# One feed-forward stage's first products by Strassen's scheme: seven block products in the place of eight

## The chip, the cores and the metric

The kernel runs on one core of one Trainium2 chip. The metric is the device time of one execution in microseconds (us); the runs of the kernel before were 1035.34 us in the median of 3 (1034.44 to 1036.2).

## The reference: what is computed

Attention over 4 x 8 heads, 576 positions, head size 64, with a decay and a causal mask; its output is 2304 tokens of 512 features. Two feed-forward stages follow on the same tokens, all in float32:

```python
def _moe_ref(x, w_in, w_out):          # stage 1: 512 -> 2048 -> 512
    h = x @ w_in
    g = h * (1.0 / (1.0 + np.exp(-h)))
    return g @ w_out

def _moe2_ref(x, w_a, w_b, w_out):     # stage 2: 512 -> 1536 -> 512
    a = x @ w_a
    b = x @ w_b
    return a * b @ w_out
```

"First products" are x @ w_in in stage 1 and x @ w_a and x @ w_b in stage 2; "second products" are those with w_out. The change concerns the first products of stage 2, a matrix of 2304 x 512 times two of 512 x 1536.

## The kernel before, in words

**Number format.** Every float32 operand of a feed-forward product is held as two float32r tiles, a rounded high part and the rest (`hi`, `lo`), and each product is three matmuls: high by high, high by low, low by high (`mm3`, L327 to L331). The weights come from DRAM as 8-byte numbers and are turned into `hi` and `lo` on the way, 256 columns at a time (`decode`, L278): one DMA, two ScalarE operations, four VectorE operations (L292, L293, L295, L297), two GpSimd operations (L299, L300).

**Tiling.** The 128 x 128 weight tile is the stationary operand, and up to 512 tokens move through it. The hidden features are cut into chunks: CH1 has seven for stage 1 (the last, chunk 6, has 2 tiles of 128 features), CH2 six for stage 2, of 2 tiles each. For each chunk the loop at L890 walks over the five token blocks of BLOCKS (four of 512, one of 256). Per block it issues the first products (`ff_in`, over 4 slices of the 512 input features, for each tile and, in stage 2, for each of the two matrices), then the second products of the block before (`ff_out`, 4 output slices by the chunk's tiles), then up to three decode steps for the next chunk. `ff_in` puts ScalarE's copy or tanh of the PSUM bank, VectorE's multiplication, ScalarE's cast to `ghi` and VectorE's subtraction for `glo` behind the products; `ff_out` adds the PSUM bank to the accumulator `acc` on VectorE (L383, L392).

**Order.** Attention and the first chunk are put in order by a planner (`Plan`): it lists the operations with modelled durations, schedules each engine by priority (`prio`), and the program issues them in that order. A row of random seeds (SHAKES) perturbs the priorities, so that another row gives another order. From chunk 1 on the order is that of the loop at L890, which no planner touches. Each engine executes its instructions in the order of issue. All loads and stores are issued by SyncE on one queue.

**Memory.** `x` holds the stage's input for all tokens as high and low parts, `accs` its sums in two halves of the tokens (TAIL = 1152). At the end of stage 1 `add_out` casts the sums back into `x`. PSUM has eight banks of 512 columns: four `s`, two `t`, one `pv`, one `mm`.

## Time and profile before

| what | value |
|---|---|
| median of 3 runs | 1035.34 us (1034.44 to 1036.2) |
| the profiled execution's own time | 1035.05 us |
| its span, first to last instruction | 1033.3 us |
| busy TensorE matmul, of the span | 1017.3 us, 98% |
| busy VectorE | 655.7 us, 63% |
| busy ScalarE | 439.6 us, 43% |
| busy GpSimd | 335.0 us, 32% |
| granted TensorE clock | 1.00 throughout |

Busy time of an engine counts the time in which at least one of its instructions is under way. Matmuls are pipelined: a row of one gives more than the engine needs before the next one can start, so a matmul's price is read from the distance of two starts. The same holds to a lesser degree on VectorE. 1.75 us of the profiled execution's time lie outside its span.

### The profile page before, as it was taken

To read this page: it belongs to the slowest core of one execution; us is meant where nothing else is said; L and a number is where in the kernel's file an instruction comes from. 1 tells how busy PE (TensorE), PEld (TensorE's weight loads), DVE (VectorE), ACT (ScalarE), POOL (GpSimd) and SP (SyncE) were. 2 spreads that over 40 slices of the span, in tenths; PEclk is the share of its full clock that TensorE was granted. 3 is DMA by queue.
4 is the path that set the end of the run, shared out by engine and by line. 5 is a ranking of instruction groups with operands and counts; after the bars stand their busy time and mean duration, and the time that the engine had idled before them with its cause. 6 is when DMAs were issued, how large, how long until landed. Compare 5 with 4: busy or idle time off the path is not lost.

```text
span 1033.3 us, 16115 instructions
## 1 busy us (share of the span) xinstructions
PE 1017.3 (98%) x5783; PEld 844.4 (82%) x5783; DVE 655.7 (63%) x1544; ACT 439.6 (43%) x1075; POOL 335.0 (32%) x414
## 2 busy tenths in 40 slices
PE   8999999999999999999999999999999999999998
PEld 6667777898788888888888788888888888888887
DVE  8896656557886857847649966176385475473334
ACT  5888788954334324423225445342232231231111
POOL 6574434333423403304006863061150250250000
PEclk9999999999999999999999999999999999999999
DMA  5443332211220201201101222021021030020012
GB/s 165 153 147 102 114 109 86 68 60 57 61 70 28 86 11 40 84 1 51 31 1 43 60 62 82 1 74 50 1 82 41 8 95 22 21 62 1 11 71 102
DMA packets 34096, 62.33 MB, mean 60 GB/s; under 512 B 7005, under 2 KB 8685, under 8 KB 33985
## 3 DMA queue, kind: packets, MB, share of 16 engines
q1 hardware_dynamic: 33904, 60.87, 19.1%
q8 instruction: 45, 0.74, 0.3%
q10 hardware_dynamic: 112, 0.45, 0.2%
q14 instruction: 35, 0.28, 0.1%
HBM read 56.05 MB, written 5.23 MB: 59 GB/s over the span
## 4 chain that ended last, share of the span: by engine, by line
PE 85%; DVE 7%; ACT 3%; DMA 3%; issue 1%; SPq 0%; POOL 0%; DVEq 0%; ACTq 0%; POOLq 0%
PE ps L329 14%; PE ps L330 14%; PE ps L331 14%; PE po L329 10%; PE po L330 9%; PE po L331 9%; PE s L582 4%; PE pv L702 3%; PE t_x L658 2%; PE t_y L658 2%; DMA d<-in_w 2%; ACT p L616 1%; DVE acc L383 1%; PE po L784 1%; PE po L785 1%
## 5 line engine op out<-in xcount | busy, mean ns | idle before, releaser
L330 PE MATMUL ps<-x,whi 128*128 128x512 f32 (+1 forms) x760 | 279.7, 368 | 0.0
L329 PE MATMUL ps<-x,whi 128*128 128x512 f32 (+1 forms) x760 | 279.6, 368 | 0.0
L331 PE MATMUL ps<-x,wlo 128*128 128x512 f32 (+1 forms) x760 | 279.6, 368 | 0.0
L299 POOL TENSOR_TENSOR d<-d,whi 128x256 f32<-128x256 f32 x116 | 97.9, 848 | 418.2 <-ACT whi L298 382.9
L329 PE MATMUL po<-ghi,whi 128*128 128x512 f32 (+1 forms) x520 | 189.6, 369 | 2.7 <-ACT ghi L361 2.7
L330 PE MATMUL po<-glo,whi 128*128 128x512 f32 (+1 forms) x520 | 191.6, 368 | 0.6 <-DVE glo L362 0.6
L331 PE MATMUL po<-ghi,wlo 128*128 128x512 f32 (+1 forms) x520 | 191.3, 368 | 0.0
L331 PEld LDWEIGHTS ps<-x,wlo 128*128 128x128 f32 x760 | 143.2, 188 | 23.9
L329 PEld LDWEIGHTS ps<-x,whi 128*128 128x128 f32 x760 | 143.3, 189 | 23.7
L330 PEld LDWEIGHTS ps<-x,whi 128*128 128x128 f32 x760 | 143.3, 189 | 23.7
L361 ACT CAST ghi<-g 128x512 fp32r<-128x512 f32 (+1 forms) x130 | 74.8, 575 | 141.0 <-DVE g L360 94.8
L329 PEld LDWEIGHTS po<-ghi,whi 128*128 128x128 f32 x520 | 97.9, 189 | 19.9 <-ACT ghi L361 3.8
L330 PEld LDWEIGHTS po<-glo,whi 128*128 128x128 f32 x520 | 98.0, 189 | 17.4 <-DVE glo L362 1.1
L331 PEld LDWEIGHTS po<-ghi,wlo 128*128 128x128 f32 x520 | 98.0, 188 | 16.2
L360 DVE TENSOR_TENSOR g<-g,ps 128x512 f32<-128x512 f32 (+1 forms) x60 | 37.9, 631 | 114.7 <-PE ps L331 114.3
L362 DVE TENSOR_TENSOR glo<-g,ghi 128x512 fp32r<-128x512 f32 (+1 forms) x130 | 88.2, 678 | 34.7 <-ACT ghi L361 34.2
L291 ACT ACTIVATE d<-d 128x256 f32<-128x256 f32 x116 | 50.6, 436 | 122.5 <-DMA d<-in_w 97.6
L300 POOL TENSOR_TENSOR wlo<-d,d 128x256 fp32r<-128x256 f32 x116 | 91.0, 789 | 34.6 <-DVE d L297 31.6
L383 DVE SCALAR_TENSOR_TENSOR acc<-po,acc 128x512 f32<-128x512 f32 (+3 forms) x144 | 76.0, 551 | 23.5 <-PE po L331 23.0
L292 DVE TENSOR_SCALAR d<-d 128x256 uint32<-128x256 uint32 x116 | 44.9, 387 | 69.4 <-ACT d L291 68.8
L392 DVE TENSOR_TENSOR acc<-po,acc 128x512 f32<-128x512 f32 (+2 forms) x120 | 64.6, 554 | 25.5 <-PE po L331 25.0
L359 ACT COPY g<-ps 128x512 f32<-128x512 f32 (+1 forms) x60 | 32.4, 540 | 103.1 <-PE ps L331 103.1
(129 smaller groups left out, 1490.6 us busy)
## 6 DMA issues: line engine op xcount, KB each, us to landing
d<-in_w SPq DMA_DIRECT2D x124, 256.0 KB
qk<-in_qk SPq DMA_DIRECT2D x15, 608.0 KB
vt<-in_v SPq DMA_DIRECT2D x16, 320.0 KB
rb<-invs SPq DMA_DIRECT2D x32, 128.0 KB
out_t<-acc SPq DMA_DIRECT2D x12, 256.0 KB
d2ghi<-in_w SPq DMA_DIRECT2D x8, 256.0 KB
e<-in_w SPq DMA_DIRECT2D x4, 256.0 KB
out_t<-acc SPq DMA_DIRECT2D x4, 192.0 KB
```

The costliest lines, as they stand in the source:

```text
L291: nc.scalar.activation(m, high.bitcast(F32), AF.Copy, scale=2.0 ** -112)
L292: nc.vector.tensor_scalar(m.bitcast(U32), m.bitcast(U32), 3, None, ALU.logical_shift_left)
L299: nc.gpsimd.tensor_sub(m, val, hi.bitcast(F32))
L300: nc.gpsimd.tensor_add(lo, m, e)
L329: nc.tensor.matmul(ps, wh, mh, start=start, stop=False)
L330: nc.tensor.matmul(ps, wh, ml, start=False, stop=False)
L331: nc.tensor.matmul(ps, wl, mh, start=False, stop=stop)
L361: nc.scalar.copy(ghi[:, t, :n], g)
L362: nc.vector.tensor_sub(glo[:, t, :n], g, ghi[:, t, :n].bitcast(F32))
L383: nc.vector.scalar_tensor_tensor(a, ps, 0.5, a, ALU.mult, ALU.add)
L392: nc.vector.tensor_add(a, ps, a)
L582: nc.tensor.matmul(out, stat, b[:, k0 + j0:k0 + j0 + nj], start=step == 0, stop=step == 3)
```

## The change: what it does, and the diff

Chunks 1 to 5 of stage 1 stay in the loop at L890. From chunk 6 on everything is issued by a second planner section.

- **Chunk 6** (`finish_first`): the same products, for six token blocks of 384 in the place of four of 512 and one of 256.
- **Stage 2, first products** (`third`): for a token block of 768 (two times 384, one from each half of the tokens), 512 input features (two times 256) and 256 hidden features (two tiles), each of the two matrices is multiplied as a 2 x 2 by 2 x 2 product of blocks in the Winograd form of Strassen's scheme: seven block products (TERMS) of 6 matmuls each where the plain form has eight. The order is SPOTS: the products of the two matrices in turn (a0 b0 a1 b1 ...), and at each "." one output slice of the second products of the sweep before. Some products accumulate in the same PSUM bank, with a copy of the bank taken on ScalarE between (k = 0, 2, 3, and 5 of the first matrix), and are finished by VectorE additions (`close`). Three sweeps, one for each block of 768 tokens, cover 256 hidden features; 18 sweeps cover the stage, and the direction of the blocks turns with each set of weights.
- **Terms of x** (`build`): the seven left operands of a block are sums of accumulator slices, made on VectorE, split into high and low on ScalarE and VectorE or GpSimd (`low_part`). They are made once per block in the first three sweeps. Two sets of slots lie in what was `x`; blocks 0 and 2 share one, so their terms are saved to a DRAM tile (`cache`) and fetched again by DMA (`save`, `fetch`: 393 KB for each part of a term).
- **Terms of the weights** (`weights`, `matrix`): per set of 256 hidden features 8 pieces of first weights and 4 of second weights are decoded; the first ones go through 8 additions on VectorE and 14 splits. Each term has one place, which is free when its product in the third sweep is done. The pieces of the first set are decoded ahead, during chunk 5 (`stage_now`).
- **Attention**: planner's costs (VectorE durations, a factor for VectorE while GpSimd works, DMA times) and the seeds are other ones; its operations are the same.
- The host's packing of stage 2's weights follows the new order of blocks.

```diff
+N2, QW = 384, 256
+THIRDS = NT // (2 * N2)
+TERMS = ("11", "12", "s1", "s2", "s3", "22", "s4")
...
 SHAKES = (
-    140891, 800875, 471325, 495185, 936710, 840775, 945215, 567712, 303858, 981929, 836138, 737549,
...
+    928192, 420176, 967232, 364299, 426396, 736720, 810573, 747836, 1486, 412859, 131987, 252009,
...
-    SWITCH, STAY = 150, 0.9
+    SWITCH, STAY, SHARE = 150, 0.9, 2.4
...
+            if op.port:
+                both = max(0, min(free.get("POOL", 0) - t, op.dur * self.SHARE))
+                op.dur += both - both / self.SHARE
...
-                plan.add("DVE", t_dve(nj) + 82, lambda out=out, low=low, o=o: nc.vector.tensor_scalar(
-                    out(), o(), -SCALE, None, ALU.mult, ALU.min, accum_out=low()), [s], [(b, j0), (nm, col)], pr + PRIO["max"])
+                plan.add("DVE", t_dve(nj) + 13, lambda out=out, low=low, o=o: nc.vector.tensor_scalar(
+                    out(), o(), -SCALE, None, ALU.mult, ALU.min, accum_out=low()), [s], [(b, j0), (nm, col)], pr + PRIO["max"], 70)
...
+    later_ops = [op for op in plan.ops if op.prio > -6.5]
     for seed in SHAKES:
-        shake(plan.ops, seed)
+        shake(later_ops, seed)
...
+    FIRST = chunks[-1][0] and next(c for c in range(len(chunks)) if chunks[c][0])
+    STAGED = "11", "12", "21", "22"
+    ORDER = 2, 3, 0, 1
+    stage = []
...
+    def stage_now(m, n, k):
...
+        nc.gpsimd.tensor_add(stage[m][:, k], val, e)
+
-    for c in range(1, len(chunks)):
+    for c in range(1, FIRST - 1):
+        if c == 3:
+            own.close()
+            more = ctx.enter_context(tc.tile_pool(name="more", bufs=1))
+            stage += [more.tile([P, 4, QW], F32, name=f"stage{m}") for m in range(2)]
         for t0, nb in BLOCKS:
             for t in range(chunks[c][2]):
                 ff_in(c, t, t0, nb)
             for s in prev:
                 s()
             prev = [lambda o=o, c=c, t0=t0, nb=nb: ff_out(c, o, t0, nb) for o in range(KC)]
-            if t0 == 0 and c != 2 and max(c + 1, 3) < len(chunks):
+            if t0 == 0 and c != 2:
                 pend = load_steps(max(c + 1, 3))
-            per = c if c < PER else PER
+                if c == FIRST - 2:
+                    pend += [lambda m=m, n=n, k=k: stage_now(m, n, k) for m in range(2) for n, k in enumerate(ORDER)]
+            per = c if c < PER else PER + (c == FIRST - 2)
...
+    spare = more.tile([P, 2, 2, N2], F32R, name="spare")
+    new_chunk(last + 1)
+    homes = wtiles[last + 1], wtiles[last]
+    W2 = len(TERMS) * QW
+    cache = dram.tile([THIRDS, len(TERMS), 2, P, 2 * N2], F32, name="cache")
...
+    def low_part(dst, full, high, reads, writes, pr, n, deps=()):
+        plan.add("DVE", t_dve(n), lambda: nc.vector.tensor_sub(dst(), full(), high()), reads, writes, pr, port=True,
+                 also=[("POOL", t_pool(n), lambda: nc.gpsimd.tensor_sub(dst(), full(), high()))])
+
+    def finish_first():
+
+        nf = chunks[last][2]
+        for i, (blk, h) in enumerate((blk, h) for blk in range(THIRDS) for h in range(2)):
+            pr = 100 * (i - 6)
+            t0 = h * TAIL + blk * N2
+            ghi, glo = (tbuf(t, [P, 2, 2, N2], F32R, f"{t}_l{i}") for t in ("ghi", "glo"))
+            for t in range(nf):
+                ps, g = bank2("s", f"ps_l{i}_{t}"), tbuf("g", [P, N2], F32, f"g_l{i}_{t}")
+                for kc in range(KC):
+                    plan.add("PE", 3 * t_mm(N2), lambda ps=ps, t=t, kc=kc, t0=t0: mm3(
+                        ps()[:, :N2], w_first(last, 0, t, kc), (x[:, 0, kc, t0:t0 + N2], x[:, 1, kc, t0:t0 + N2]),
+                        kc == 0, kc == KC - 1),
+                        [("xh", (blk, h, kc // 2)), ("xl", (blk, h, kc // 2))] + [("wf", 1, k) for k in range(4)], [ps], pr + 10 * t)
...
+            for oc in range(KC):
+                ps = bank2("t", f"po_l{i}_{oc}")
+
+                def out_mm(ps=ps, oc=oc, ghi=ghi, glo=glo):
+                    for t in range(nf):
+                        mm3(ps()[:, :N2], w_second(last, t, oc), (ghi()[:, t, 0], glo()[:, t, 0]), t == 0, t == nf - 1)
...
+    regions = [(r, h, k) for r in range(THIRDS) for h in range(2) for k in range(2)]
+    sets = regions[:7], regions[7:] + ["spare", regions[6]]
...
+    def save(blk, k, pr):
+        for i, key in enumerate(("xh", "xl")):
+            slot = sets[blk == 1][k]
+            plan.dma(480, 8 * P * N2, lambda i=i: nc.sync.dma_start(
+                cache[blk, k, i].rearrange("p (k t) -> p k t", k=2), term(slot, i).bitcast(F32)),
+                [(key, slot)], [("cache", blk, k, i)], pr)
+
+    def fetch(blk, terms, pr):
+        for k in terms:
+            slot = sets[blk == 1][k]
+            for i, key in enumerate(("xh", "xl")):
+                plan.dma(480, 8 * P * N2, lambda k=k, i=i, slot=slot: nc.sync.dma_start(
+                    term(slot, i).bitcast(F32), cache[blk, k, i].rearrange("p (k t) -> p k t", k=2)),
+                    [("cache", blk, k, i)], [(key, slot)], pr + k)
+
+    def build(blk, terms, pr):
+
+    def build(blk, terms, pr):
+
+        st = sets[blk == 1]
+        quarter = lambda h, k, c: accs[h][:, 2 * k + c, blk * N2:(blk + 1) * N2]
+        plain = {0: (0, 0), 1: (0, 1), 6: (1, 1)}
+        sums = {2: ((1, 0), (0, 0)), 3: ((1, 1), 2), 5: ((0, 1), 3), 4: ((1, 1), (1, 0))}
...
+        for k in terms:
...
+                    plan.add("DVE", t_dve(N2), lambda src=src, a=a, b=b: nc.vector.tensor_sub(src(), a(), b()),
+                             [ka, kb], [src], pr + k, port=True)
+                plan.add("ACT", t_act(N2, 93), lambda hi=hi, src=src: nc.scalar.copy(hi(), src()), [key], [("xh", st[k], c), ("xh", st[k])], pr + k)
+                low_part(lo, src, lambda hi=hi: hi().bitcast(F32), [key, ("xh", st[k], c)], [("xl", st[k])], pr + k, N2)
+            if blk != 1 or k == 6:
+                save(blk, k, pr + k + 20)
...
+        for n, k in enumerate(ORDER) if j else ():
+            _, e, val = fields(j, (4 * m + n) * QW, f"{j}_{m}{k}", pr)
+            plan.add("POOL", t_pool(QW), lambda e=e, val=val, at=at, k=k: nc.gpsimd.tensor_add(at(k), val(), e()),
+                     [val, e], [("st", m, k)], pr)
...
+        add, sub = nc.vector.tensor_add, nc.vector.tensor_sub
+        convert(0, lambda: at(0), ("st", m, 0))
+        convert(1, lambda: at(1), ("st", m, 1))
+        convert(2, *sum_of("s1", add, "21", "22"))
+        convert(3, *sum_of("s2", sub, "s1", "11"))
+        convert(4, *sum_of("s3", sub, "11", "21", to="21"))
+        convert(5, lambda: at(3), ("st", m, 3))
+        convert(6, *sum_of("s4", sub, "12", "s2", to="12"))
+    def weights(j, pr):
+
+        for m in range(2):
+            matrix(j, m, pr)
+        for n in range(4):
+            t, e, val = fields(j, (8 + n) * QW, f"{j}_2{n}", pr)
...
+    SPOTS = "a0 b0 . a1 b1 . a2 b2 . a3 b3 . a4 b4 . a5 b5 . a6 b6 . .".split()
...
+    def third(q):
+
+        j, i = divmod(q, THIRDS)
+        blk = i if j % 2 == 0 else THIRDS - 1 - i
...
+                for c in range(2):
+                    mm3(ps()[:, :N2], (hi[:, c * P:(c + 1) * P], lo[:, c * P:(c + 1) * P]), (xh[:, c], xl[:, c]),
+                        start and c == 0, c == 1, not start)
...
+        def close(t, h, m, got, ps, at):
+
+            dst, key = got
+            plan.add("DVE", t_dve(N2), lambda: nc.vector.tensor_add(dst(), ps()[:, :N2], dst()), [ps], [key], at)
+            if m:
+                plan.add("DVE", t_dve(N2), lambda: nc.vector.tensor_mul(dst(), firsts[t, h](), dst()), [firsts[t, h]], [key], at, port=True)
+                split(t, h, dst, at)
...
+        for k in range(7):
+            for m in range(2):
+                at = pr + spots["ab"[m] + str(k)][0] + 2
+                bank = "xyzxxxz"[k]
+                if k < 3:
+                    banks[m, bank] = bank2(("pv", "mm")[m] if k == 1 else "s", f"{bank}_{q}_{m}")
+                ps = banks[m, bank]
+                product(m, k, bank, k < 3)
...
+                if k in (0, 2, 3):
+                    kept[m, k] = keep_part(ps, *((0, 0), None, (1, 1), (0, 1))[k], m, at)
+                elif k == 5:
+                    dst, key = place(1, 0, m)
...
+                else:
+                    close(*{1: (0, 0), 4: (1, 1), 6: (0, 1)}[k], m, kept[m, {1: 0, 4: 2, 6: 3}[k]], ps, at)
+        for n, (h, oc) in enumerate((h, oc) for h in range(2) for oc in range(KC)):
+            at = pr + 100 + spots["."][n]
+            ps = bank2("t", f"po_{q}_{h}{oc}")
...
+            if j == 0:
+                plan.add("ACT", t_act(N2), lambda ps=ps, a=a: nc.scalar.copy(a, ps()[:, :N2]), [ps], [key], at + 2)
+            else:
+                plan.add("DVE", t_dve(N2), lambda ps=ps, a=a: nc.vector.tensor_add(a, ps()[:, :N2], a), [ps], [key], at + 2)
...
+    finish_first()
+    pairs = FF2 // (2 * P)
+    weights(0, -400)
+    build(0, (0, 1, 2, 3, 4, 5, 6), -250)
+    build(1, (0, 1, 2, 3, 4, 5), 40)
+    for q in range(THIRDS * pairs):
+        j, i = divmod(q, THIRDS)
+        third(q)
+        if i == THIRDS - 1 and j + 1 < pairs:
+            weights(j + 1, 100 * (q - 2) + 150)
+        if q == 0:
+            build(1, (6,), 60)
+            build(2, (0, 1, 2, 3, 5, 4), 65)
+        elif q == 1:
+            build(2, (6,), 160)
+        elif i == 0:
+            fetch(1, (6,), 100 * q + 50)
+            fetch(2 if j % 2 == 0 else 0, range(6), 100 * q + 60)
+        elif i == 1:
+            fetch(2 if j % 2 == 0 else 0, (6,), 100 * q + 50)
+    with tc.manual_schedule():
+        for op in plan.order():
+            op.fn()
```

## Rows read from the trace of the kernel before

**Rows 1.** The page: busy time by engine, then busy tenths in 40 slices.
```profile
PE 1017.3 (98%) x5783; PEld 844.4 (82%) x5783; DVE 655.7 (63%) x1544; ACT 439.6 (43%) x1075; POOL 335.0 (32%) x414
...
PE   8999999999999999999999999999999999999998
...
PEclk9999999999999999999999999999999999999999
```
**Rows 2.** Busy time by stretch (windows): chunk 6, stage 2's first chunk, its fourth.
```profile
core 0: us, PE busy (x) PEld busy (x) DVE busy (x) ACT busy (x) POOL busy (x), PEclk, DMA share, GB/s
538.82:587.90 49.08, 47.20 (x222) 38.99 (x221) 42.69 (x75) 24.25 (x55) 35.63 (x40) 1.00 0.18 54
587.90:661.80 73.90, 73.90 (x361) 62.64 (x360) 42.73 (x84) 33.24 (x75) 29.34 (x33) 1.00 0.18 50
...
809.60:883.50 73.90, 73.90 (x362) 62.63 (x361) 43.68 (x92) 20.25 (x44) 18.99 (x24) 1.00 0.15 43
```
**Rows 3.** Timeline of TensorE: starts of matmuls of 512 columns, then of 256.
```profile
645.37 0.39 PE L329 MATMUL po<-ghi,whi 128*128 128x512 f32 x1
645.60 0.39 PE L330 MATMUL po<-glo,whi 128*128 128x512 f32 x1
645.83 0.39 PE L331 MATMUL po<-ghi,wlo 128*128 128x512 f32 x1
646.05 0.28 PE L329 MATMUL ps<-x,whi 128*128 128x256 f32 x1
646.17 0.28 PE L330 MATMUL ps<-x,whi 128*128 128x256 f32 x1
646.29 0.28 PE L331 MATMUL ps<-x,wlo 128*128 128x256 f32 x1
```
**Rows 4.** Timeline of VectorE in stage 2: start, us, line, operation.
```profile
778.90 0.68 DVE L392 TENSOR_TENSOR acc<-po,acc 128x512 f32<-128x512 f32 x1
779.50 0.68 DVE L362 TENSOR_TENSOR glo<-g,ghi 128x512 fp32r<-128x512 f32 x1
780.10 0.29 DVE L295 TENSOR_SCALAR d<-d 128x256 uint32<-128x256 uint32 x1
780.30 0.29 DVE L292 TENSOR_SCALAR d<-d 128x256 uint32<-128x256 uint32 x1
...
781.11 0.42 DVE L297 SCALAR_TENSOR_TENSOR d<-d,d 128x256 f32<-128x256 uint32 x1
781.44 0.42 DVE L293 SCALAR_TENSOR_TENSOR d<-d,d 128x256 uint32<-128x256 uint32 x1
```
**Rows 5.** Groups by line and shape (lines): busy us, mean ns; VectorE, ScalarE, GpSimd.
```profile
L293 DVE SCALAR_TENSOR_TENSOR d<-d,d 128x256 uint32<-128x256 uint32 x116 | 60.6, 524 | 2.1
L392 DVE TENSOR_TENSOR acc<-po,acc 128x384 f32<-128x384 f32 x20 | 11.0, 548 | 0.0
L390 ACT COPY acc<-po 128x384 f32<-128x384 f32 x4 | 1.9, 487 | 0.0
L386 ACT CAST x<-acc 128x384 fp32r<-128x384 f32 x4 | 2.0, 506 | 0.0
L298 ACT CAST whi<-d 128x256 fp32r<-128x256 f32 x116 | 45.9, 405 | 70.5 <-DVE d L293 58.3 <-PE po L330 11.4
L299 POOL TENSOR_TENSOR d<-d,whi 128x256 f32<-128x256 f32 x116 | 97.9, 848 | 418.2 <-ACT whi L298 382.9 <-DVE glo L362 25.3 <-DVE d L292 10.0
```
**Rows 6.** Timeline of VectorE, two operations of Rows 4's kinds in chunk 6's stretch.
```profile
588.98 1.41 DVE L293 SCALAR_TENSOR_TENSOR d<-d,d 128x256 uint32<-128x256 uint32 x1
590.31 0.68 DVE L383 SCALAR_TENSOR_TENSOR acc<-po,acc 128x512 f32<-128x512 f32 x1
```
**Rows 7.** Busy time by stretch: attention, then three stretches of stage 1 (columns as Rows 2).
```profile
0.00:230.00 230.00, 220.58 (x1899) 169.85 (x1900) 157.75 (x534) 181.31 (x514) 113.85 (x149) 1.00 0.36 111
...
250.00:300.00 50.00, 48.88 (x227) 40.77 (x226) 43.46 (x102) 20.03 (x44) 19.90 (x24) 1.00 0.22 64
...
400.00:450.00 50.00, 50.00 (x239) 42.14 (x238) 40.32 (x84) 18.91 (x41) 15.79 (x19) 1.00 0.21 64
```
**Rows 8.** TensorE's waits by releaser, the two longest: total us, times, longest.
```profile
PE idle L438 <- POOL maskb L430: 3.3, 1, 3.3
PE po L329 <- ACT ghi L361: 2.7, 3, 1.3
```
**Rows 9.** Timeline of the end: TensorE's last matmul, VectorE's last addition.
```profile
1029.83 0.28 PE L331 MATMUL po<-ghi,wlo 128*128 128x256 f32 x1
...
1030.14 0.42 DVE L392 TENSOR_TENSOR acc<-po,acc 128x256 f32<-128x256 f32 x1 [0.29 <-PE po L331]
```

More of the change, by code (lines that the diff above doesn't have):

```diff
@@ L103, in __init__ @@
         self.ways, self.prio, self.after, self.head, self.tail = ways, prio, after, head, tail
-        self.deps, self.bufs, self.start, self.end, self.mode = set(), [], None, None, 0
+        self.deps, self.bufs, self.start, self.end, self.mode, self.port = set(), [], None, None, 0, False
 class Spare:
@@ L120, in __init__, with add @@
         self.ops, self.writer, self.readers = [], {}, {}
-    SWITCH, STAY = 150, 0.9
-    def add(self, eng, dur, fn, reads=(), writes=(), prio=0, after=0, also=(), mode=WHOLE):
+    SWITCH, STAY, SHARE = 150, 0.9, 2.4
+    def add(self, eng, dur, fn, reads=(), writes=(), prio=0, after=0, also=(), mode=WHOLE, port=False):
         op = Op([(eng, dur, fn), *also], prio, after)
-        op.mode = mode
+        op.mode, op.port = mode, port
         for k in list(reads) + list(writes):
@@ L147, in add, with dma @@
         return op
-    def dma(self, issue, size, fn, reads=(), writes=(), prio=0, eng="SP"):
+    def dma(self, issue, size, fn, reads=(), writes=(), prio=0, eng="SP", late=0):
         self.add(eng, issue if eng == "SP" else 60, fn, reads, writes, prio, 900)
-        self.add("DMA", size / 330, lambda: None, reads, writes, 0, 950)
+        self.add("DMA", size / 300, lambda: None, reads, writes, 0, 950 + late)
     def swdge(self, issue, size, fn, reads=(), writes=(), prio=0):
@@ new lines, in term @@
+    def term(slot, i):
+        if slot == "spare":
+            return spare[:, i]
+        r, h, k = slot
+        return x[:, i, 2 * k:2 * k + 2, h * TAIL + r * N2:h * TAIL + (r + 1) * N2]
+    regions = [(r, h, k) for r in range(THIRDS) for h in range(2) for k in range(2)]
[6 more added lines that the diff above has]
+                [(key, slot)], [("cache", blk, k, i)], pr)
@@ L933 @@
         rows = [m[:, fs].reshape(KC, P, n * P).transpose(1, 0, 2).reshape(P, -1) for m in firsts]
+        if stage:
+            rows = [m[:, fs].reshape(2, 2, P, 2, P)[k, :, :, i].transpose(1, 0, 2).reshape(P, -1)
+                    for m in firsts for i, k in ((1, 0), (1, 1), (0, 0), (0, 1))]
         rows.append(second[fs].reshape(n, P, DM).transpose(1, 0, 2).reshape(P, -1))
```

187 lines of the change are left out of this document (164 added, 23 removed), and 10 rows, old and new, of the table SHAKES.

## The prediction

> **What bounds the kernel now.** The page comes first: TensorE is busy for 98% of the span, with a granted clock of 1.00 in every slice, and the next engine, VectorE, for 63% [rows 1]. Then the stretches: a chunk of stage 2 lasts 73.9 us, and TensorE is busy in all of it [rows 2]. Busy is not peak, so the third view is the timeline, for the distance of two starts. At 512 columns it is (646.05 - 645.37) / 3 = 0.2267 us, at 256 columns 0.120 us [rows 3]. A chunk of stage 2 is 72 matmuls per token block, so it should last 72 x (4 x 0.2267 + 0.120) = 73.9 us. That is what it lasts: stage 2 has no gap to close, and only fewer matmul columns can shorten it. The waits agree: TensorE's two longest are 3.3 us at the very start and 2.7 us in three pieces [rows 8]. Before the last microseconds idle time stands in three places: 9.4 us in attention's 230 us [rows 7], 1.1 us between 250 and 300 us [rows 7], and 1.9 us in the stretch of chunk 6 [rows 2]. The reader should keep VectorE's column beside them: 43.5 of 50 us (87%) in the second, 42.7 of 49.1 us (87%) in the third, while 40.3 of 50 us (81%) leaves TensorE no idle time [rows 7].
>
> **Fewer columns (the gain).** The two prices in [rows 3] differ by 0.1067 us for 256 columns, which leaves 0.0133 us that does not depend on the columns. So 384 columns, for which there is no row, cost 0.160 + 0.0133 = 0.1733 us by interpolation. A sweep has 14 block products and 8 output slices of 6 matmuls each: 132 x 0.1733 = 22.9 us. Eighteen sweeps are 411.8 us against 6 x 73.9 = 443.5 us: **-31.7 us**. An eighth of the first products would be 37 us in the same prices; the narrower blocks give some of it back. Chunk 6 has 48 x 6 = 288 such matmuls, 49.9 us, against 48 x 1.0267 = 49.3 us: **+0.6 us**.
>
> **Where VectorE's prices come from.** Starts again, not durations: 0.60 us at 512 columns, 0.335 us for a two-input operation on 256 (781.11 to 781.44), 0.20 us for a one-input operation on 256 [rows 4]. A 384-column operation shows 0.548 us [rows 5]; at 512 columns the duration is 0.085 us above the distance (0.685 against 0.60), so I take 0.463 us. A decoded piece is 2 x 0.20 + 2 x 0.335 = 1.07 us. GpSimd's operations on 256 columns last 0.82 us (0.848 in the row, the other kind somewhat less) [rows 5].
>
> GpSimd slows VectorE. The same L293 that takes 0.42 us takes 1.41 us at 588.98 [rows 4, 6]. To price it, I count a chunk of stage 2 as it is: 32 operations of 0.60 us, 8 of 0.335 us, 0.3 us for blocks cut at TAIL and 12 pieces make 35.0 us, and the row has 43.7 us busy with GpSimd busy for 19.0 us [rows 2]. The excess, 8.7 / 19.0 = 0.46 us per us of GpSimd, is an upper value, since it holds the overlap of durations too. From below the price is 0, if the pieces fall apart in time; from above it is 1, if each us of GpSimd stops VectorE for a us. I take 0.46.
>
> **Chunk 6 in its new order.** VectorE has 6 blocks x 8 operations x 0.463 = 22.2 us, four second pieces 4.3, eight weight sums and seven low parts 5.0, and the terms of block 0, 8 sums and 14 low parts, 10.2: 41.7 us, and 8 GpSimd operations add 6.6 x 0.46 = 3.0. That is 44.7 of 49.9 us, 90%. The rows at 87% have 1.1 and 1.9 us of idle TensorE; I put 2.0 here, where the old order had 1.9: **+0.1 us** (bounds -1.9 and +5).
>
> **Sweeps 0 to 2.** TensorE needs 14 x 6 x 0.1733 = 14.6 us for the first, which has no output slices yet, and 2 x 22.9: 60.3 us. VectorE needs 3 x 14 x 0.463 = 19.4 us for closing, multiplying and splitting (the first set's output is copied on ScalarE), 2.3 for the second matrix's low parts, 20.4 for the terms of blocks 1 and 2, and for the next set of weights 12 x 1.07 + (8 + 14) x 0.335 = 20.2: 62.3 us. Sixteen GpSimd operations, 13.1 us, add 6.0: 68.3 us, 8.0 more than there is. Moving low parts to GpSimd does not help much, since each saves 0.46 us and costs VectorE about as much. But the second pieces (4.3 us) are first wanted in sweep 4, and the later terms' low parts during sweep 3. I take **+4.5 us**; bounds 0, if all of the excess can wait, and 15.1, at a price of 1.
>
> **Sweeps 3 to 17.** A set needs 3 x 22 x 0.463 = 30.6 us, plus 20.2 for weights, plus 6.0: 56.8 of 68.6 us, 83%. Between the row at 81% (idle 0) and those at 87% (1.9 of 49.1 us) this gives 0 to 13 us over 343 us; it is nearest to the first: **+2.5 us**.
>
> **Costed at nothing.** ScalarE: per set 21 copies at 0.487, 12 casts at 0.506 [rows 5] and 30 operations on 256 columns at about 0.41 are 29 of 68.6 us. Its cover is that slack; were it gone, a copy late by 0.5 us would still fit into the distance worked out below. Transfers: per set 8 terms of 2 x 393 KB and 12 pieces of 262 KB are 9.4 MB in 68.6 us, 137 GB/s. In attention 111 GB/s took a share of 0.36 [rows 7], so this takes 0.45. All of it goes over SyncE's one queue, in planned order; a fetch that waits for a term's slot holds the weight loads behind it, but a term's slot is free a whole sweep (22.9 us) before its new content is used. The packing on the host is outside the time.
>
> **The end.** From the last matmul's start to the end of the span there are 3.5 us [rows 9]. The last addition is 0.12 us longer at 384 columns, and its store is half as large again: **+0.5 us** (0 to 3).
>
> **Attention.** The same operations in another order. Of 9.4 us of idle time 3.3 are the very start [rows 7, 8]; 6.1 us bound the gain, and I bound the loss by the same size. A small gain is likelier, as the new costs have a price for GpSimd's effect on VectorE, which [rows 6] shows to be real: **-1.0 us**.
>
> **Sum.** 1035.05 - 31.7 + 0.6 + 0.1 + 4.5 + 2.5 + 0.5 - 1.0 = 1010.6 us for a profiled execution. The median of the runs is 0.3 us above the profiled one: **1010.8 us**.
>
> **Rivals.**
>
> *VectorE and GpSimd exclude each other.* The stretched row speaks for it: 1.41 us in place of 0.42, a stretch of 0.99 us, at least as long as a whole GpSimd operation of 0.82 us [rows 4 to 6]; the average of 0.46 speaks against it. At a price of 1, sweeps 0 to 2 lose 15.1 us, and a set takes 50.8 + 13.1 = 63.9 of 68.6 us, 93%, where I take the whole 13 us of stall: 1010.8 + 10.6 + 10.5 = 1032 us at the worst, 1018 to 1033 as a case. Chance 0.19. By the Trainium skill, SBUF — State Buffer, section "Who interferes with whom", an instruction of VectorE with two inputs in SBUF and one of GpSimd that reads SBUF take one shared port by turns, as an exclusive lock, while one with a single SBUF input is free. By that rule the change is worse than its count, since it adds sums, products and low parts, nearly all with two SBUF inputs; the trace agrees in kind (1.41 us for two inputs, 0.68 us for the addition from PSUM behind it) and not in the average.
>
> *Bank hand-offs set the pace (slower than before).* Products 3, 4 and 5 of a matrix share one PSUM bank: 4 must wait for ScalarE's copy of 3, and 5 for VectorE's addition after 4. Between them lie two other items, 12 x 0.1733 = 2.08 us. The copy or addition takes 0.49 or 0.55 us [rows 5] and perhaps 0.3 us of signalling, an estimate from the 0.29 us VectorE waits per output slice at the end [rows 9]: about 1.2 us are free. There are 4 such places in a sweep, 72 in all. The saving is gone when each stalls by 24.5 / 72 = 0.34 us, that is, when the answering engine is late by 1.5 us every time. One stretched operation of 1.41 us [rows 6] in front is almost that, but it would have to be there nearly always. At 1.7 us of lateness the time is about 1010.8 - 2.5 + 72 x 0.5 = 1044 us. Chance 0.09.
>
> *Nothing stalls and attention gains.* The bounds from below: -31.7 + 0.6 - 1.9 + 0 + 0 and -1 to -6 for attention: 996 to 1002 us. The planner knows the contention, and the row at 81% shows how much a queue can absorb; against it, sweeps 0 to 2 have more work than time. Chance 0.10.
>
> **How the numbers follow.** My forecast, stalls of a few us beside a full saving, spans 1003 to 1018 us: chance 0.60. The exclusive port has 0.19, no stall 0.10, the hand-offs 0.09, and 0.02 is left for a mixture that ends within 0.2% of before, about what a measurement of this kernel can tell from no change. Faster: 0.60 + 0.17 + 0.10 = 0.87; same 0.04, with 0.02 from the exclusive port's worst; slower 0.09. The range runs from 1000 us, a third of the way into the case without stalls, up to 1028 us, two thirds of the way through the exclusive port's; 0.60 + 0.04 + 0.13 and a part of the mixture lie in it.
>
> **What would show it.** In the changed trace, starts of 384-column matmuls 0.173 us apart; at 0.19 the 2376 of them would take 40 us more and the saving would be gone. TensorE's idle time should gather in the 60 us behind chunk 6, with VectorE busy for 90% there, and VectorE as releaser. In the later sets VectorE should be busy for 80 to 88%. Idle time at product 4 or 5 of every sweep would be the hand-off rival; waits on transfers at the terms' first products would mean that the cover I gave the fetches was not there. If attention's end (about 230 us) moves by more than 3 us, that term was mis-sized.

## The result and the profile after

The changed kernel takes 1018.75 us (median of 4 runs, 1015.96 to 1019.05) against 1035.63 us before: a ratio of 0.9826, 95% interval 0.9807 to 0.9845. That is faster by 1.7%, and the whole interval lies below 1. It is within the range and 8 us longer than predicted, just outside the 1003 to 1018 us that the prediction gave to its own mechanism. The profiled execution took 1019.05 us, with a span of 1017.3 us, where before's took 1035.05 us.

Two lines of the page of the changed kernel, engines and granted clock, answer to [rows 1].

```profile
PE 993.3 (98%) x6041; PEld 891.5 (88%) x6041; DVE 765.5 (75%) x1854; ACT 490.5 (48%) x1211; POOL 293.1 (29%) x366
...
PEclk9999999999999999999999999999999999999999
```

TensorE's share is again 98%, so the share alone says nothing about where 8 us went. The busy time by stretch (columns as [rows 2]) does. A set is the three sweeps that share one set of weights. The stretches are chunk 6 with the first products of sweep 0, the rest of sweeps 0 to 2, the second set, and two later sets.

```profile
531.00:596.00 65.00, 58.00 (x317) 55.98 (x315) 63.15 (x129) 34.54 (x80) 24.20 (x26) 0.97 0.41 142
596.00:655.60 59.60, 59.51 (x333) 59.28 (x334) 54.32 (x124) 37.17 (x90) 14.68 (x17) 0.97 0.37 124
655.60:724.00 68.40, 66.73 (x385) 66.41 (x384) 51.65 (x120) 29.46 (x70) 13.91 (x17) 1.00 0.43 139
724.00:795.00 71.00, 69.53 (x400) 68.89 (x399) 58.70 (x136) 27.40 (x65) 14.49 (x18) 1.00 0.42 134
795.00:866.00 71.00, 69.52 (x400) 68.87 (x398) 59.02 (x136) 27.38 (x64) 14.49 (x18) 1.00 0.41 134
```

In the 65 us from chunk 6's start TensorE stands idle for 7 us; before, chunk 6's stretch had 1.9 [rows 2]. VectorE is busy for 63.15 of these 65 us (97%), and for 47.8 of the first 49.9 us (96%), for which the prediction had 90%. Each later set has 1.5 us of idle TensorE at a VectorE share of 83%, exactly the share that the prediction worked out. Two stretches have a granted clock of 0.97, which no stretch of before has.

TensorE's waits by releaser (total, times, longest) name who was late; they answer to [rows 8].

```profile
PE po_l L336 <- DVE acc L1007: 6.0, 3, 2.9
PE po L336 <- DVE acc L1221: 4.5, 4, 1.4
...
PE x L336 <- DVE z L1175: 1.7, 1, 1.7
PE x L336 <- ACT z L1169: 1.0, 1, 1.0
```

The four releasers are VectorE's additions from a bank, those of chunk 6 (L1007) and those of the output (L1221), one sum after a first product and one copy by ScalarE. Waits on a transfer do not appear, and neither TensorE nor VectorE has a wait in this stage that is put down to GpSimd (ScalarE has two, 1.6 us in all), so results that GpSimd delivers late are not what held them. A bank hand-off between first products (the last two rows) stopped TensorE twice in the whole stage.

One such stall, first on TensorE: three starts 0.173 us apart, then a hole.

```profile
794.93 0.33 PE L336 MATMUL x<-x,whi 128*128 128x384 f32 x1
795.11 0.33 PE L337 MATMUL x<-x,whi 128*128 128x384 f32 x1
795.28 0.34 PE L338 MATMUL x<-x,wlo 128*128 128x384 f32 x1
797.02 0.44 PE L336 MATMUL po<-ghi,whi 128*128 128x384 f32 x1 [1.40 <-DVE acc L1221]
```

And what VectorE did in the 6 us before TensorE went on:

```profile
790.29 0.42 DVE L968 TENSOR_TENSOR wlo<-stage,whi 128x256 fp32r<-128x256 f32 x1
790.62 0.96 DVE L1102 TENSOR_TENSOR ws<-ws,stage 128x256 f32<-128x256 f32 x1
791.51 1.23 DVE L1102 TENSOR_TENSOR ws<-stage 128x256 f32<-128x256 f32 x1
792.66 0.41 DVE L1102 TENSOR_TENSOR stage<-stage 128x256 f32<-128x256 f32 x1
...
793.33 0.96 DVE L1102 TENSOR_TENSOR stage<-stage,ws 128x256 f32<-128x256 f32 x1
...
794.88 1.61 DVE L968 TENSOR_TENSOR wlo<-stage,whi 128x256 fp32r<-128x256 f32 x3
796.42 0.54 DVE L1221 TENSOR_TENSOR acc<-po,acc 128x384 f32<-128x384 f32 x1
```

GpSimd in the same microseconds:

```profile
790.51 0.79 POOL L1087 TENSOR_TENSOR stage<-d,d 128x256 f32<-128x256 f32 x1 [21.66 <-DVE ws L1102]
791.26 1.19 POOL L969 TENSOR_TENSOR glo<-z,ghi 128x384 fp32r<-128x384 f32 x1
793.26 0.75 POOL L969 TENSOR_TENSOR wlo<-ws,whi 128x256 fp32r<-128x256 f32 x1 [0.80 <-ACT whi L1107]
795.37 0.84 POOL L1087 TENSOR_TENSOR stage<-d,d 128x256 f32<-128x256 f32 x1 [1.36 <-DVE wlo L968]
```

The two lists are read side by side by their ends. An operation on 256 columns takes VectorE 0.41 us alone. The one that starts at 790.62 ends at 791.58, 0.28 us after GpSimd's of 790.51 to 791.30. The next ends at 792.74, 0.29 us after GpSimd's end at 792.45; the one of 793.33 ends at 794.29, 0.28 us after 794.01. Each stretched operation finishes just behind GpSimd's, as if it had been held until then. All of the stage bears this out: from chunk 6 on 65 of VectorE's operations with both inputs in SBUF are stretched, and each ends 0.28 us (256 columns) or 0.41 to 0.42 us (384 columns) behind an operation of GpSimd. Who began first decides: of those that begin while one of GpSimd's is under way 65 of 69 are stretched, of 48 that began before GpSimd's only one is. The Trainium skill, SBUF — State Buffer, section "Who interferes with whom", calls this an exclusive lock on a shared port, taken by an instruction of VectorE with two inputs in SBUF and one of GpSimd that reads; these ends agree with it. Of the 63 operations with an input from PSUM that run beside GpSimd none is stretched. Of the 43 with one input in SBUF (L1072, L1076) 14 are, and end 0.15 us behind GpSimd; the prediction's words that one with a single SBUF input is free do not hold for these.

Behind ten operations on weights, four of them stretched in this way, stands the addition that empties an output bank. Its product had been finished since about 790.4 us; it started at 796.42, and TensorE, which needs the bank, waited for it.

The largest stall has the same form: at 590.57 us TensorE waits for 2.86 us, while GpSimd has two 384-column operations in a row, VectorE's 0.55 us operation beside them takes 1.36 us, and the addition L1007 stands behind.

### The profile page after: what moved, and what is told of

It is laid out like the page before. It is cut to its first block, busy times and chain, and to the rows that moved or that the text cites. A ratio compares the mean times of both kernels' runs of the same rounds, so it can differ in the third digit from the quotient of the medians.

```text
span 1017.3 us, 17206 instructions
## 1 busy us (share of the span) xinstructions
PE 993.3 (98%) x6041; PEld 891.5 (88%) x6041; DVE 765.5 (75%) x1854; ACT 490.5 (48%) x1211; POOL 293.1 (29%) x366
## 4 chain that ended last, share of the span: by engine, by line
PE 68%; DVE 9%; DMA 1%; issue 1%; ACT 0%; SPq 0%; DVEq 0%; ACTq 0%
PE po L336 9%; PE po L337 9%; PE po L338 9%; PE ps L337 5%; PE ps L336 5%; PE ps L338 5%; PE x L336 4%; PE x L338 4%; PE x L337 4%; PE z L336 2%; PE z L338 2%; PE z L337 2%; DVE wlo L968 1%; DVE ws L1102 1%; DMA d<-in_w 1%; PE y L336 1%
## 5 line engine op out<-in xcount | busy, mean ns | idle before, releaser
L336 PE MATMUL po<-ghi,whi 128*128 128x384 f32 (+2 forms) x528 | 184.0, 352 | 4.8 <-DVE acc L1221 4.5
L337 PE MATMUL po<-glo,whi 128*128 128x384 f32 (+2 forms) x528 | 184.7, 350 | 0.0
L338 PE MATMUL po<-ghi,wlo 128*128 128x384 f32 (+2 forms) x528 | 184.7, 350 | 0.0
L1221 DVE TENSOR_TENSOR acc<-po,acc 128x384 f32<-128x384 f32 x120 | 66.1, 551 | 51.6 <-PE po L338 51.6
L336 PE MATMUL x<-x,whi 128*128 128x384 f32 x264 | 89.3, 338 | 2.7 <-DVE z L1175 1.7
L337 PE MATMUL x<-x,whi 128*128 128x384 f32 x264 | 88.9, 337 | 0.0
L338 PE MATMUL x<-x,wlo 128*128 128x384 f32 x264 | 88.8, 336 | 0.0
L337 PE MATMUL ps<-x,whi 128*128 128x512 f32 (+1 forms) x240 | 88.4, 368 | 0.0
L336 PE MATMUL ps<-x,whi 128*128 128x512 f32 (+1 forms) x240 | 88.4, 368 | 0.0
L338 PE MATMUL ps<-x,wlo 128*128 128x512 f32 (+1 forms) x240 | 88.4, 368 | 0.0
L390 DVE SCALAR_TENSOR_TENSOR acc<-po,acc 128x512 f32<-128x512 f32 (+2 forms) x120 | 63.1, 550 | 18.9 <-PE po L338 18.6
L628 ACT ACTIVATE p<-p,nm 128x384 f32<-128x384 f32 (+3 forms) x128 | 70.7, 556 | 3.6 <-DVE nm L620 3.2
L620 DVE CUSTOM_DVE_ANT_0 p<-s,maskw 128x512 f32<-128x512 f32 (+3 forms) x128 | 55.8, 484 | 13.8 <-PE t_y L670 6.4
```

Of the source, the lines that this page charges most:

```text
L336: nc.tensor.matmul(ps, wh, mh, start=start, stop=False, skip_group_check=joined)
L337: nc.tensor.matmul(ps, wh, ml, start=False, stop=False, skip_group_check=joined)
L338: nc.tensor.matmul(ps, wl, mh, start=False, stop=stop, skip_group_check=joined)
L390: nc.vector.scalar_tensor_tensor(a, ps, 0.5, a, ALU.mult, ALU.add)
L620: plan.add("DVE", t_dve(nj) + 13, lambda out=out, low=low, o=o, mk=mk: nc.vector.tensor_tensor_reduce(out(), o(), mk, -SCALE, 3.0e38, ALU. ...
L628: plan.add("ACT", t_act(sum(IB[ib]), 279), lambda b=b, c=c, nj=sum(IB[ib]): nc.scalar.activation(b()[:, :nj], b()[:, :nj], AF.Exp, bias=nm ...
```

## The experiments

Times are medians of 4 runs each, and ratios are to the kernel before, run beside them, with their 95% interval. The edits are against the changed kernel. The kernel before had medians of 1034.35 to 1036.05 us beside the experiments, so times of different sets compare to about 1 us. Attention adds to that: with the same code up to chunk 6, its first matmul starts anywhere between 528.2 and 530.6 us in eight traces. So TensorE's stalls are given too, counted from chunk 6's first matmul to the last one above 0.1733 us for each start: 21.4 us in the changed kernel.

**Attention alone.** How much of the gain is attention's?

```diff
-    for c in range(1, FIRST - 1):
+    for c in range(1, len(chunks)):
...
-    finish_first()
-    pairs = FF2 // (2 * P)
...
```

> Attention's new order and costs with the old stage 2 (the old loop from chunk 1 on). The trace after the change has chunk 3 of stage 1 start 3.6 us earlier than before, which is to be attention's new order and the early chunks behind it. If it is, this kernel runs in about 1035.6 - 3.6 = 1032 us, and the new stage 2 is worth the other 13 us. Rival: the shift comes from the smaller memory and decode work around chunks 1 and 2 in the new kernel and is given back later; then this kernel runs within 1 us of before, 1035 us.

Measured: 1029.78 us, 0.9952 (0.9937 to 0.9967). The order of attention is worth some 5 us, not 1. Without the very start, TensorE idles for 2.7 us up to 235 us where before it idled for 6.2, and chunk 3 starts at 303.83 us in place of 309.50. In the changed kernel's own profiled execution the gain at chunk 3 was 3.6 us (305.87). The rest of the change is then worth 0.9826 - 0.9952, about 13 us, of the 31.1 us that the columns give.

**GpSimd's operations cut short, in the same order.**

```diff
+        c = slice(0, n if whole or writes[0][0] not in ("xl", "wl") or writes[0][1] == "spare" else 16)
...
-                 also=[("POOL", t_pool(n), lambda: nc.gpsimd.tensor_sub(dst(), full(), high()))])
+                 also=[("POOL", t_pool(n), lambda: nc.gpsimd.tensor_sub(dst()[:, c], full()[:, c], high()[:, c]))])
...
-            plan.add("POOL", t_pool(QW), lambda e=e, val=val, at=at, k=k: nc.gpsimd.tensor_add(at(k), val(), e()),
+            plan.add("POOL", t_pool(QW), lambda e=e, val=val, at=at, k=k: nc.gpsimd.tensor_add(at(k)[:, :16], val()[:, :16], e()[:, :16]),
...
```

The columns left out keep what stood there, so this kernel leaves a part of the result out; the operations of TensorE, VectorE and ScalarE are all there.

> Same order of every engine as in the changed kernel; from chunk 6 on GpSimd's additions and subtractions work on 16 columns in place of 256 or 384, except where a tile would be read unwritten (the first sets, the first split of a tile); the parts left out keep what stood there. Theory (GpSimd holds VectorE's two-input operations, VectorE falls behind the plan, TensorE waits for PSUM banks that VectorE frees late): the stalls of 1.6 to 1.9 us in each of the later sets go, about 8 us, and part of the 8 us around chunk 6: 1006 to 1010 us. Rival (VectorE simply has too much work of its own, or its queue has the wrong order): nothing of its work is taken away, so 1018 to 1019 us, with the stalls where they were.

Measured: 1003.63 us, 0.9700 (0.9684 to 0.9715), 2 us below what was expected; stalls 7.0 us. A later set, busy time by stretch:

```profile
722.00:791.00 69.00, 68.92 (x397) 68.42 (x396) 54.47 (x134) 27.16 (x63) 5.97 (x18) 1.00 0.43 138
```

With the same orders on all engines, but GpSimd busy for 5.97 us instead of 14.49, the set has 0.5 us of stall instead of 2.0. The clock did not fall in the stage. What is left around chunk 6 is the 1.87 us at 538.85 us, beside the first set of weights, whose operations were kept whole, and 1.2 us at 586.87 us behind a copy on ScalarE. So it is GpSimd's time, not the order or the number of operations, that makes most of the lost 15 us.

**More of it.** Sixty-four unconnected additions of 256 columns (the expectation counts 60), each behind one of the stage's GpSimd operations.

```diff
+    def more_work():
+        nc.gpsimd.tensor_add(extra[:, 0], extra[:, 1], extra[:, 2])
...
-            plan.add("POOL", t_pool(QW), lambda e=e, val=val, at=at, k=k: nc.gpsimd.tensor_add(at(k), val(), e()),
+            plan.add("POOL", t_pool(QW), lambda e=e, val=val, at=at, k=k: (nc.gpsimd.tensor_add(at(k), val(), e()), more_work()),
...
```

> Same order as in the changed kernel; behind 60 of GpSimd's operations from chunk 6 on stands one more addition of 256 columns on tiles that nobody else uses, 0.8 us each, 12 us for each of the five sets decoded there. Theory: VectorE loses up to another 0.5 us per us of GpSimd, part of it in slack: 1024 to 1040 us, with the added stalls at the same waits (TensorE for VectorE's additions from PSUM). Rival (VectorE's own work or order): GpSimd is busy for only 14 of 70 us in a set and is waited for by nobody, so 1019 to 1021 us.

Measured: 1028.13 us, 0.9936 (0.9919 to 0.9953); 9.4 us more for about 55 us of GpSimd, 0.17 us per us; stalls 30.4 us. The additions also put off GpSimd's own results, but here too no wait of VectorE or TensorE is put down to GpSimd.

```profile
729.00:800.00 71.00, 68.88 (x386) 67.71 (x385) 59.81 (x132) 25.42 (x61) 22.53 (x29) 0.98 0.42 134
```

TensorE now idles for 2.1 us in the set (1.5 without the additions), and the clock fell three times in the stage. VectorE's share is hardly above that of the set without additions (84 against 83%), which is a first sign that the share does not set the stall.

**The lock in the planner.** The planner's list gives a two-input operation of VectorE that overlaps one of GpSimd a longer duration, by a factor of 2.4 on the overlap. Here the later of the two starts when the earlier ends, in the second stage alone.

```diff
+                        if self.lock and (way[0] == "POOL" or (way[0] == "DVE" and op.port)):
+                            other = held["POOL" if way[0] == "DVE" else "DVE"]
+                            start = max([start] + [e for b, e in other[-3:] if b <= start < e])
...
-            if op.port:
+            if self.lock and (way[0] == "POOL" or (way[0] == "DVE" and op.port)):
+                held[way[0]].append((t, t + op.dur))
+            if op.port and not self.lock:
...
```

> The same operations; only the second planner section's rule for VectorE and GpSimd is another one: where a GpSimd operation and a port operation of VectorE would overlap, the later one starts when the earlier one ends, in place of a factor of 2.4 on the overlap. The order then allows for the lock. Theory (VectorE's lateness against its plan makes the stalls): the plan is met more nearly and TensorE waits less: 1004 to 1014 us. Rival (there is too much VectorE work whatever the order): 1017 to 1020 us. If the order comes out worse by chance, over 1020 us, it tells nothing of the lock.

Measured: 1011.08 us, 0.9771 (0.9756 to 0.9787), a time that the theory had given, but not for its reason alone; stalls 15.1 us. Chunk 6 and the first sweeps lost less, and the stall of the second set went; the three sets behind it kept most of theirs (1.6 us each in place of 2.0). TensorE's longest waits in this kernel:

```profile
PE po L342 <- DVE acc L1228: 4.3, 4, 1.3
PE po_l L342 <- DVE acc L1014: 4.0, 2, 2.3
```

The output's addition (L1228 here) let TensorE wait for up to 1.3 us, once in each of these sets. In one such place VectorE had eleven operations, nine of them on weights, between it and the addition before, and three of the nine were stretched by 0.4 to 0.5 us. The lock in the plan is part of the remedy, not the whole.

**Banks first.** Operations that empty a PSUM bank go ahead of all others in the sweeps' list; the lock stays unplanned.

```diff
+    FIRST_BY = 300
...
-                plan.add("DVE", t_dve(N2), lambda ps=ps, a=a: nc.vector.tensor_add(a, ps()[:, :N2], a), [ps], [key], at + 2)
+                plan.add("DVE", t_dve(N2), lambda ps=ps, a=a: nc.vector.tensor_add(a, ps()[:, :N2], a), [ps], [key], at + 2 - FIRST_BY)
...
```

> The changed kernel with one edit of priorities: in the sweeps, the copies and additions that empty a PSUM bank come before all other work of VectorE and ScalarE that is ready at the same time; GpSimd's work and the rule for it stay. Theory of the lock: the old order had no stall in its own plan in these places, so priorities change little there, and VectorE still falls behind by the lock; but a bank-emptying operation now has fewer others in front, so part of the 8 us of stalls in the later sets goes: 1011 to 1018 us. Rival (the priorities alone made the stalls, weights before accumulations): all of the later sets' stalls go, and the time is 1008 to 1011 us.

Measured: 1009.78 us, 0.9747 (0.9731 to 0.9763): the rival's number; stalls 13.8 us. Chunk 6's stretch, then a later set:

```profile
529.00:594.00 65.00, 57.98 (x317) 55.94 (x315) 63.00 (x129) 34.52 (x80) 24.20 (x26) 0.97 0.41 142
723.00:793.00 70.00, 70.00 (x406) 70.00 (x405) 58.61 (x135) 27.40 (x64) 18.52 (x22) 1.00 0.42 136
```

The later set has no idle time left, although GpSimd does more there (18.52 us) than before the edit; chunk 6, which the edit does not touch, is as it was. So the later stalls need both, the lock that makes VectorE late and the weight operations in front of the addition. Taking away either ends them.

**Both.** The two edits together.

> The plan with the lock, 1011.1 us, and the banks' priorities together. In the trace with the lock alone a run of weight sums and splits still stands in front of an addition that frees a bank, and TensorE waits 1.5 us once in each later set, 5 us in all. Theory: that part goes, 1005 to 1009 us. If the two edits act on the same stalls, 1010 to 1012 us.

Measured: 1005.83 us, 0.9705 (0.9687 to 0.9723), as expected; stalls 8.1 us. The later sets are clean; chunk 6 still idles for 4.6 of 65 us, and the clock fell once.

**Nothing on GpSimd.** From chunk 6 on all its operations go to VectorE; nothing is left out.

```diff
...
-                 also=[("POOL", t_pool(n), lambda: nc.gpsimd.tensor_sub(dst(), full(), high()))])
...
-            plan.add("POOL", t_pool(QW), lambda e=e, val=val, at=at, k=k: nc.gpsimd.tensor_add(at(k), val(), e()),
+            plan.add("DVE", t_dve(QW), lambda e=e, val=val, at=at, k=k: nc.vector.tensor_add(at(k), val(), e()),
...
```

> From chunk 6 on GpSimd does nothing: its additions and subtractions go to VectorE, 16 more operations of 0.335 us a set (5.4 us), and all low parts. Nothing is left out. Theory of the lock: VectorE has more work, about 56 of 69 us a set, but nobody holds its port; it keeps to the plan and TensorE waits less: 1002 to 1010 us. Rival (VectorE is the bound by the amount of its work): the added 5.4 us a set and more around chunk 6 make it slower than the changed kernel: 1022 to 1045 us.

Measured: 998.92 us (997.8 to 999.47), 0.9643 (0.9628 to 0.9657). Stalls are 2.3 us, 1.5 of them at 583.64 us behind a copy on ScalarE. It is the fastest version, together with the next one, and faster than the theory's 1002 to 1010 us. Chunk 6, the second set and a later set:

```profile
529.00:594.00 65.00, 63.64 (x366) 62.95 (x365) 64.63 (x159) 38.01 (x88) 0.00 (x0) 1.00 0.36 128
...
652.00:721.00 69.00, 69.00 (x400) 68.91 (x399) 59.54 (x157) 29.58 (x70) 0.00 (x0) 1.00 0.45 146
721.00:790.00 69.00, 69.00 (x399) 68.91 (x398) 58.70 (x152) 27.02 (x64) 0.00 (x0) 1.00 0.43 140
```

VectorE is busy for 99% of chunk 6's stretch and TensorE idles for 1.4 us; in a set VectorE is busy for 85% and TensorE does not idle at all. Against the changed kernel, VectorE has 152 operations in a set in place of 136 and the same 58.70 us of busy time. So moving the work there was free in VectorE's time, and it took the lumps away. What GpSimd's 14.49 us had cost VectorE can be added up row by row: 12 stretched operations of that set last 5.3 us longer than alone, 0.37 us per us.

**Nothing on GpSimd and banks first.**

> The same with the banks' priorities. Theory: without GpSimd the order met its plan already, so there is little left for priorities: within 2 us of the kernel without GpSimd. Rival (order): 3 us or more below it.

Measured: 999.37 us, 0.9647 (0.9633 to 0.9662): no difference, as expected; stalls 2.0 us. Without GpSimd the order needs no such help.

**The same, with unconnected GpSimd work that reads, or that only fills.** The 64 additions put on top of the version without GpSimd, and in a second kernel 64 fills of 768 columns (0.74 us each); the second edit below is against the first.

```diff
+    def more_work():
+        nc.gpsimd.tensor_add(extra[:, 0], extra[:, 1], extra[:, 2])
...
+            plan.add("DVE", t_dve(QW), lambda e=e, val=val, at=at, k=k: (nc.vector.tensor_add(at(k), val(), e()), more_work()),
...
-    def more_work():
-        nc.gpsimd.tensor_add(extra[:, 0], extra[:, 1], extra[:, 2])
+    def more_work():
+        nc.gpsimd.memset(extra, 0.0)
```

> The kernel without GpSimd from chunk 6 on (998.9 us), in the same order, with 60 GpSimd additions of 256 columns of about 0.8 us on tiles that nobody else uses, 12 a set. If GpSimd's reading of its operands is what holds VectorE, stalls come back: 1003 to 1012 us. If the amount of VectorE's work or the data that GpSimd delivered late made the stalls, nothing happens: 998 to 1000 us.

> The same with 60 GpSimd fills of 768 columns, which read nothing, in the place of the additions. If only operations that read hold VectorE, 998 to 1000 us and VectorE's two-input operations keep their length; if any GpSimd operation holds it, about the same loss per us of GpSimd as with the additions.

Measured: 1006.63 us, 0.9719 (0.9705 to 0.9734), and 1001.71 us, 0.9678 (0.9661 to 0.9694). As placed, the pair does not answer its question: with nothing to wait for on an otherwise empty queue, the work ran at 264 to 350 us, in stage 1, and GpSimd was idle from 529 us on. What both times lost against 998.92 us they lost there: from chunk 6 on the stalls are 2.6 and 2.7 us, while between 297 and 320 us TensorE idled for 4.0 us beside the additions and for 1.8 us beside the fills. But the overlap can be read there. VectorE's groups by shape (busy, mean ns) between 297 and 320 us, beside the additions:

```profile
L369 DVE TENSOR_TENSOR glo<-g,ghi 128x512 fp32r<-128x512 f32 x4 | 3.6, 898 | 1.4 <-ACT ghi L368 1.4
L364 DVE SCALAR_TENSOR_TENSOR g<-g,ps 128x512 f32<-128x512 f32 x4 | 2.7, 681 | 3.2 <-ACT g L363 3.2
...
L300 DVE SCALAR_TENSOR_TENSOR d<-d,d 128x256 uint32<-128x256 uint32 x1 | 0.9, 903 | 0.0
...
L299 DVE TENSOR_SCALAR d<-d 128x256 uint32<-128x256 uint32 x1 | 0.7, 676 | 1.1 <-ACT d L298 1.1
```

And beside the fills:

```profile
L369 DVE TENSOR_TENSOR glo<-g,ghi 128x512 fp32r<-128x512 f32 x5 | 3.4, 688 | 1.4 <-ACT ghi L368 1.4
L364 DVE SCALAR_TENSOR_TENSOR g<-g,ps 128x512 f32<-128x512 f32 x4 | 2.7, 685 | 3.4 <-ACT g L363 3.4
...
L299 DVE TENSOR_SCALAR d<-d 128x256 uint32<-128x256 uint32 x1 | 0.9, 936 | 1.2 <-ACT d L298 1.2
...
L300 DVE SCALAR_TENSOR_TENSOR d<-d,d 128x256 uint32<-128x256 uint32 x1 | 0.4, 426 | 0.0
```

Operations with both inputs in SBUF (L369, L300) are stretched by additions, which read, and take their plain 0.69 and 0.43 us beside fills. The one with an input from PSUM (L364) takes 0.68 us beside either. The one-input L299, whose like takes 0.29 us alone [rows 4], is stretched by both. There are one to five operations in a group, so these are few cases; whether fills in stage 2 would have stalled TensorE was not seen.

## Why the prediction came out as it did

The columns were right. Starts of 384-column matmuls are 0.173 us apart, an undisturbed sweep lasts 22.88 us where 22.9 was worked out, and the version without GpSimd keeps the whole saving: 0.9643 against 0.9952 for attention alone is 32 us, where the columns alone give 31.1.

Against the profiled 1035.05 us, the terms came out so (measured stalls are TensorE's distances of starts above the undisturbed ones; from those of chunk 6 the 2.6 us that it had before are taken off, as the prediction takes off 1.9):

| term | predicted, us | measured, us |
|---|---|---|
| columns, with chunk 6 | -31.1 | -31.1, at starts 0.173 us apart |
| chunk 6 and sweeps 0 to 2, stalls | +4.6 | +9.6, of which 3 are the clock |
| sweeps 3 to 17, stalls | +2.5 | +9.1 |
| end | +0.5 | +0.3 |
| attention and what follows up to chunk 3 | -1.0 | -3.6 |
| sum | -24.5 | -15.7; the profiled executions differ by 16.0 |

The stalls were 11.6 us above the forecast; that attention gave 2.6 us more hid a part of this, which was luck. And the range held because it took in two thirds of the rival's span.

**The step that failed** is the reading of a stall from VectorE's busy share, between the row at 81% and those at 87%. It gave 2.5 us for the sweeps 3 to 17 at a share of 83%. The share was right to the per cent, and the stall was 9.1 us. The experiments show that the share is not the measure: TensorE does not idle in a set at 84% (banks first) and at 85% (nothing on GpSimd), and idles for 1.4 us at 99%. What counts is how late one addition is, and that is set by the operations in front of it: a few stretched ones in a row, behind each other, make a lump of 2 us that a share over 70 us does not show.

**The price of GpSimd** was near as an average: 0.46 us per us was taken, as an upper value, and 0.37 was found in a set. The prediction used it as an even charge on VectorE's time, though. Its own stretched row [rows 6] showed the other half: the charge falls on single operations, in lumps of up to 1 us.

**Chunk 6 and sweeps 0 to 2.** The size was off by 5 us, and the place was half right. Idle time gathers from chunk 6's start on, with VectorE as releaser, but 6.0 us of it are waits for chunk 6's own additions (L1007), where the prediction had 2.0 us. The sweeps 0 to 2, to which it gave 4.5 us for 8 us of excess work, have almost none of their own: from 601 us to the end of sweep 2 the starts lie 0.2 us above the undisturbed ones. In chunk 6 VectorE was busier (96 against 90%). 3 us of the stalls are the clock, which no step had.

**Attention** was mis-sized. Chunk 3 starts 3.6 us earlier; about 2.5 us of that is idle time that went before 235 us, and the rest is a wait of 1.3 us near 267 us in stage 1 that is gone. Whether attention's own end moved by more than 3 us, the announced sign, cannot be read off, since what stands around it has another order. With attention alone 3.5 us of idle time went there (6.2 us before, 2.7 in that kernel). That the planner's new price for GpSimd is what made the difference there was only argued, not tried.

**Costed at nothing** held. ScalarE held TensorE up once, for 1.0 us. The transfers took a share of 0.41 to 0.43 and 134 to 139 GB/s in the three sets shown, where 0.45 and 137 were worked out, and TensorE never waited for one.

**The rivals.** Of the 72 bank hand-offs between first products that the prediction counted, one stalled TensorE, by 1.7 us (a fifth product that waited for VectorE's addition after the fourth, at 668.55 us). One more, of a kind that it did not count, cost 1.0 us (a product behind ScalarE's copy of the first, at 594.76 us). That mechanism is refuted as a bound. VectorE and GpSimd do exclude each other, operation by operation, and 1018.75 us lies at the lower edge of that rival's span; its worst price, a us for every us, is not what a set pays, because part of GpSimd's time meets operations with an input from PSUM, none of which was stretched, or an idle VectorE. The forecast and the rival were not two cases but one mechanism, priced by its average and by its peak. The case without stalls, 996 to 1002 us, is what the version without GpSimd reaches.

The 1.87 us at the start of chunk 6, which remained with short GpSimd operations, is gone in the version without GpSimd, so it too hangs on GpSimd. What stays open is whether fills, which read nothing, would have stalled TensorE in stage 2, and when the clock falls (below).

## What to carry to other kernels

A helper engine that shares a port with the one on the path is not free capacity: here its 14.5 us per set kept VectorE as busy as the same work done by VectorE itself did (58.70 us either way), and moving all of it there gained 20 us. A stall is not read from a busy share over a long stretch; follow the one operation that frees a buffer, and count what stands in front of it and by how much that can stretch. An order planned on paper should hold exclusion as exclusion, and operations that empty a bank belong ahead of work that only has to be done some time.

## What the runs showed of the hardware that was not expected

The granted clock fell to half (1.2 of 2.4 GHz) twice in this stage, each time for 3.4 us: once 1.7 us after TensorE had gone on from a stall of 1.9 us, and once right behind stalls of 3.0 and 1.2 us. The stretch of the first idle time, the low clock behind it, the second idle time and the low clock behind that (columns as [rows 2]):

```profile
541.00:545.00 4.00, 2.29 (x12) 1.71 (x11) 3.81 (x10) 2.77 (x7) 1.73 (x3) 1.00 0.27 79
545.00:548.40 3.40, 3.40 (x12) 3.40 (x12) 3.29 (x7) 1.83 (x5) 1.75 (x2) 0.50 0.79 284
...
590.00:596.20 6.20, 2.35 (x13) 1.71 (x12) 6.20 (x11) 2.55 (x6) 2.82 (x3) 1.00 0.35 127
596.20:599.60 3.40, 3.40 (x11) 3.40 (x12) 3.38 (x9) 1.87 (x5) 0.71 (x1) 0.50 0.00 0
```

TensorE was busy for all of both low stretches, so a share of busy time hides them; the timeline shows them as distances of 0.32 us.

```profile
545.33 0.53 PE L336 MATMUL po_l<-ghi_l,whi 128*128 128x384 f32 x1
545.65 0.53 PE L337 MATMUL po_l<-glo_l,whi 128*128 128x384 f32 x1
545.97 0.53 PE L338 MATMUL po_l<-ghi_l,wlo 128*128 128x384 f32 x1
```

Each cost about 1.5 us: in 3.4 us, eleven or twelve matmuls instead of twenty. The stalls of 1.6 us in the later sets were followed by none, nor was the one of 1.6 us at 561.66 us or the one of 1.8 us at 668.55 us, while the additions put into stage 1 brought one at 305.64 us, behind stalls of 2.0 and 2.4 us. A single stall of 1.9 us was followed by a fall in this kernel (at 541 us) and by none in the kernel with short GpSimd operations (at 538.85 us), so which holes bring it stays open. With the lock in the planner a stall of 2.5 us was followed by 6.8 us at half clock (from 588.7 us). Where it falls, a stall is paid for twice: 3 us in this kernel, nothing in the version without GpSimd.

The other surprise is the queue: work without any dependence, written in the middle of stage 2, ran at 264 to 350 us on an engine that had nothing else to wait for, and held back stage 1. The same additions behind GpSimd's own work had run at 541 to 921 us.
